# A builder that schedules the TensorE stream, with four PSUM banks shared by all tasks, in a kernel of four interleaved layers

## The chip, the cores and the metric

The kernel runs on one core of one Trainium2 chip. The metric is the device time of one execution, in microseconds (us); smaller is better. Engines are named as in the profile: PE is TensorE (PEld its weight loads), ACT is ScalarE, DVE is VectorE, POOL is GpSimd, SP issues transfers. Ratios are taken to runs of the kernel before on the same chip in the same rounds. The experiments ran on three chips, on which the kernel before took 3972, 3964 and 3957 us, so stage times of different traces, and medians, can differ by 0.4% for that reason alone.

## The reference, cut to what matters

The reference is four residual layers over 2048 rows of 512: A, B, A, B, each behind a layer norm.

```python
x = x + A(layernorm(x)); x = x + B(layernorm(x))
x = x + A(layernorm(x)); x = x + B(layernorm(x))

# A: 64 segments of 32 rows, 32 heads of 128, a memory of 8 rows handed on
for s in range(64):
    h = concat([mem, xs])                     # 40 rows
    q, k, v = h @ Wq, h @ Wk, h @ Wv          # each 32 heads x 128
    o = softmax(mask(q k^T * scale)) v @ Wo
    mem = o[:8]; outs.append(o[8:])           # the next segment needs mem

# B: full attention, 32 heads of 16, 2048 x 2048 scores a head
o = softmax(q k^T * 0.25) v @ wo
```

A segment of A is a chain that ends in the memory of the next, so there are 128 segments one after the other. A layer B has no such chain: as soon as A has left a few hundred rows, some of B's scores can be computed. The kernel cuts B into *units* (4 to 16 score matmuls, the exp, as many matmuls with V) and puts them between the tasks of the A segments. Units that are left when A has ended form a *tail*; between the two A layers a short *interlude* waits for B.

## The kernel before

One segment is 22 tasks in a fixed order. Q and K are projections of eight heads each, V of 1024 columns, S the scores and their exp, T the transposed probabilities, P the product with V, W the output projection. Each task fills one PSUM bank (P fills two, and all four W one), and an engine then copies the bank to SBUF. The Trainium skill, "PSUM — Partial Sum Buffer" (Specifications (TRN2)), gives eight banks of 512 fp32 values a partition; the pools below add up to eight (2 + 3 + 2 + 1).

```python
def psum_main(self, st):
    ...
    self.psA = self.pool("psA", bufs=2, space=PSUM)              # A tasks, projections: two banks
    psS = self.pool("psS", bufs=1, space=PSUM)
    self.SX = psS.tile([128, 3, 512], f32, name="b_SX")          # score columns 0 to 2 of a unit
    self.SY = [psS.tile([128, 512], f32, name=f"b_SY{i}") for i in range(2)]   # column 3
    self.oacc = psS.tile([128, 512], f32, name="b_oacc")

def psum_tail(self, st):                                         # layout of the tail
    ...
    self.psA = self.pool("psT", bufs=1, space=PSUM)
    self.SH = [psS.tile([128, 2, 512], f32, name=f"b_SH{i}") for i in range(3)]
    ...

def emit_qk(self, u):                                            # a unit: scores, then exp
    ...
    if self.tail:
        h = [self.SH[(2 * n) % 3], self.SH[(2 * n + 1) % 3]]
        ex = [(0, 2, h[0][:, 0:2, 0:w]), (2, 4, h[1][:, 0:2, 0:w])]
    else:
        y = self.SY[n % 2]
        ex = [(0, 3, self.SX[:, 0:3, 0:w]), (3, 4, y[:, 0:w])]
    ...

PLAN = "Q0 K0 Q1 K1 S0 Q2 K2 Q3 K3 S1 V0 V1 V2 T0 V3 T1 P0 P1 W0 W1 W2 W3".split()

def segment(self, A, s):
    quota = min(13, -(-self.backlog // 4)) if s % 4 == 0 else self.quota   # units in this segment
    self.act_evac = quota < 6        # light: Q, V and half of P copied by ACT, else by DVE
    for step in self.PLAN:
        ...                          # emit the task, then a unit or other work when it is due
```

Of the kernel before, what the change touches and what calls it, by code (L numbers as in the profile page):

```python
# [18 lines left out]
SEG = 32  # L19
M = 8  # L20
# [10 lines left out]
FORCE_GENERAL = False  # L31


class Kern:
    def __init__(self, ctx, tc, T):
        self.ctx, self.tc, self.nc, self.T = ctx, tc, tc.nc, T
        self.misc, self.outq, self.tqq = deque(), deque(), deque()
        self.runs, self.next = [], deque()
        self.cur = None
        self.pending = []  # L40
        self.backlog = 0
        self.acc_wait, self.acc_open = deque(), 0
        self.n_units = 0
        self.k_cache, self.v_cache = {}, {}
        self.act_evac = True
        self.tail = False
# [100 lines left out]
    def psum_main(self, st):  # L147
        self.ctx, outer = st, self.ctx
        self.psA = self.pool("psA", bufs=2, space=PSUM)
        psS = self.pool("psS", bufs=1, space=PSUM)  # L150
        self.SX = psS.tile([128, 3, 512], f32, name="b_SX")
        self.SY = [psS.tile([128, 512], f32, name=f"b_SY{i}") for i in range(2)]
        self.oacc = psS.tile([128, 512], f32, name="b_oacc")
        self.nc.vector.memset(self.oacc[:], 0.0)
        self.ctx = outer

    def psum_tail(self, st):
        self.ctx, outer = st, self.ctx
        self.tail = True
        self.psA = self.pool("psT", bufs=1, space=PSUM)  # L160
        psS = self.pool("psU", bufs=1, space=PSUM)
        self.SH = [psS.tile([128, 2, 512], f32, name=f"b_SH{i}") for i in range(3)]
        self.oacc = psS.tile([128, 512], f32, name="b_oaccT")
        self.nc.vector.memset(self.oacc[:], 0.0)
        self.ctx = outer
# [18 lines left out]
    def set_flag(self):  # L184
        nc = self.nc
        ps = self.psA.tile([1, 128], f32, name="flagT", tag="a")
        nc.tensor.transpose(ps[:], self.okm[:], self.identf[:])
        m = self.sm_p.tile([1, 1], f32, name="flagm")
        nc.vector.tensor_reduce(m[:], ps[:], axis=AX.X, op=ALU.min)
        nc.vector.tensor_scalar(m[:], m[:], -1.0, 1.0, op0=ALU.mult, op1=ALU.add)  # L190
        nc.vector.tensor_copy(self.flag[:], m[:])
# [16 lines left out]
    def transposes(self, xn, name):  # L208
        pt = self.psA.tile([128, 4, 128], bf16, name=name, tag="a")
        for ft in range(4):  # L210
            self.nc.tensor.transpose(pt[:, ft, :], xn[:, ft * 128:(ft + 1) * 128], self.ident[:])
        return pt


    def run_misc(self):
        if len(self.tqq) > 2 and self.tqq[0] is None:
            self.tqq.popleft()
        for q in (self.tqq, self.outq, self.misc):
            if q:
                f = q.popleft()  # L220
                if f is not None:
                    f()
                    return

    def flush_out(self):
        while self.outq:
            f = self.outq.popleft()
            if f is not None:
                f()
# [14 lines left out]
    def slot(self, unit=True):  # L244
        u = None
        if unit:
            self.commit()
            if self.next:
                u = self.next.popleft()
                self.backlog -= 1  # L250
                self.emit_qk(u)
                self.pending.append(u)
        if u is None and self.backlog == 0 and self.pending:
            self.pv_run()
        elif len(self.pending) >= 3:
            self.pv_run()
        self.run_misc()
        self.commit()
        for nu in list(self.next)[0:4]:
            self.load(nu)  # L260
        return u is not None

    def emit_qk(self, u):
        nc = self.nc
        self.load(u)
        assert u.run.q is not None and u.k is not None
# [4 lines left out]
        n = self.n_units  # L271
        self.n_units += 1
        if self.tail:
            h = [self.SH[(2 * n) % 3], self.SH[(2 * n + 1) % 3]]
            out = [h[0][:, 0, :], h[0][:, 1, :], h[1][:, 0, :], h[1][:, 1, :]]
            ex = [(0, 2, h[0][:, 0:2, 0:w]), (2, 4, h[1][:, 0:2, 0:w])]
        else:
            y = self.SY[n % 2]
            out = [self.SX[:, 0, :], self.SX[:, 1, :], self.SX[:, 2, :], y[:]]
            ex = [(0, 3, self.SX[:, 0:3, 0:w]), (3, 4, y[:, 0:w])]  # L280
# [4 lines left out]
        for a, b, src in ex:  # L285
            dst = pt[:, a:b, 0:w] if b - a > 1 else pt[:, a, 0:w]
            nc.scalar.activation(dst, src, ACT.Exp, scale=B_SCALE)  # L287

    def pv_run(self):
        u = self.pending.pop(0)  # L290
        self.pv_mm(u)
        if not u.last and self.pending:
            u = self.pending.pop(0)
            self.pv_mm(u)

    def pv_mm(self, u):
        qw = u.run.qw
        nj = len(u.kjs)
        for j, kj in enumerate(u.kjs):
# [3 lines left out]
        if u.last:  # L303
            u.run.close()

    def load(self, u):
        nc = self.nc
        run = u.run
        B = run.B
        if run.q is None:  # L310
            run.q = self.qp.tile([128, 512], bf16, name="b_q")
# [4 lines left out]
        if u.k is None:  # L316
# [15 lines left out]
            for w in run.units:  # L332
                if w.piece == u.piece:
                    w.k, w.v = self.k_cache[key], self.v_cache[key2]
# [8 lines left out]
    def drain_until(self, cond):  # L343
        while not cond():
            assert self.backlog or self.misc or self.outq or self.tqq or self.pending
            self.slot()


    def ln_chunk(self, x_src, ck, dt):
# [5 lines left out]
        def pe():  # L355
            pt = self.transposes(xn, "a_lnT")
            r0 = (4 * ck) % RING
            nc.vector.tensor_copy(self.hT[:, :, L * r0:L * (r0 + 4)].rearrange("p f (g q) -> p f g q", q=L)[:, :, :, 0:SEG],
                                  pt[:].rearrange("p f (g q) -> p f g q", q=SEG))
        return pe  # L360

    def qk_group(self, h_s, proj, g, ft_major=False):
        nc = self.nc
        W = self.Wq if proj == 0 else self.Wk
        ps = self.psA.tile([128, 8, L], f32, name="a_qk", tag="a")
        order = [(u, ft) for ft in range(4) for u in range(8)] if ft_major else [(u, ft) for u in range(8) for ft in range(4)]
        for n, (u, ft) in enumerate(order):
            h = 8 * g + u
            nc.tensor.matmul(ps[:, u, :], lhsT=W[:, ft, h * DH:(h + 1) * DH], rhs=h_s[:, ft, 0:L],  # L369
                             start=(n == 0) if ft_major else (ft == 0), stop=(ft == 3), skip_group_check=ft_major)  # L370
        if proj == 0:
            dst = self.QT[:, 8 * L * g:8 * L * (g + 1)].rearrange("p (u q) -> p u q", q=L)
            if self.act_evac:
                nc.scalar.copy(dst, ps[:])  # L374
            else:
                nc.vector.tensor_copy(dst, ps[:])  # L376
        else:
            nc.vector.tensor_copy(self.KT[:, 8 * g:8 * g + 8, :], ps[:])  # L378

    def v_round(self, h_s, r):  # L380
        nc = self.nc
        ps = self.psA.tile([128, 512], f32, name="a_v", tag="a")
        for ft in range(4):
            for ct in range(2):
                n = 2 * r + ct
                nc.tensor.matmul(ps[64 * ct:64 * ct + 64, :], lhsT=h_s[:, ft, :], rhs=self.Wv[:, ft, n * 512:(n + 1) * 512],  # L386
                                 start=(ft == 0), stop=(ft == 3), tile_position=(0, 64 * ct))
        if self.act_evac:
            nc.scalar.copy(self.V[:, r, :], ps[:])  # L389
        else:  # L390
            nc.vector.tensor_copy(self.V[:, r, :], ps[:])  # L391

    def s_group(self, s, st):
        nc = self.nc
        ps = self.psA.tile([128, 8, L], f32, name="a_s", tag="a")
        for hp in range(8):
            for ct in range(2):
                h = 2 * (8 * st + hp) + ct
                nc.tensor.matmul(ps[64 * ct:64 * ct + 64, hp, :], lhsT=self.QT[:, L * h:L * h + 64], rhs=self.KT[:, h, :], start=True, stop=True, tile_position=(0, 64 * ct))  # L399
        pn = self.pn[:, st, :, 0:L]  # L400
        nc.scalar.activation(pn, ps[:], ACT.Exp, scale=A_SCALE)  # L401
        nc.vector.tensor_tensor(self.pn[:, st, :, 0:SEG], self.pn[:, st, :, 0:SEG], self.mask[:], ALU.mult)
        sm = self.smA[:, s % 16, 8 * st:8 * st + 8]
        nc.vector.reduce_sum(sm, pn, axis=AX.X)
        r = self.sm_p.tile([128, 8, 1], f32, name="a_r")
        nc.vector.reciprocal(r[:, :, 0], sm)
        nc.vector.tensor_tensor(pn, pn, r[:].to_broadcast([128, 8, L]), ALU.mult)

    def pt_group(self, pti):
        nc = self.nc  # L410
        ps = self.psA.tile([128, 8, L], f32, name="a_pt", tag="a")
        for ii in range(8):
            r, h4 = divmod(8 * pti + ii, 4)
            for ct in range(2):
                h = 4 * (2 * r + ct) + h4
                hp, cs = divmod(h, 2)
                nc.tensor.matmul(ps[64 * ct:64 * ct + 64, ii, :], lhsT=self.pn[:, hp // 8, hp % 8, :], rhs=self.sel[cs], start=True, stop=True, tile_position=(0, 64 * ct))
        nc.vector.tensor_copy(self.PT[:, pti, :, :], ps[:])  # L418

    def pv_group(self, gi):  # L420
        nc = self.nc
        ps = [self.psA.tile([128, 8, L], f32, name=f"a_o{ct}", tag="a") for ct in range(2)]
        for r2 in range(2):
            for h4 in range(4):
                for ct in range(2):
                    r = 2 * gi + r2
                    nc.tensor.matmul(ps[ct][:, 4 * r2 + h4, :], lhsT=self.V[64 * ct:64 * ct + L, r, h4 * DH:(h4 + 1) * DH],  # L427
                                     rhs=self.PT[64 * ct:64 * ct + L, gi, 4 * r2 + h4, :], start=True, stop=True, tile_position=(64 * ct, 0))
        dst = self.OT[:].rearrange("p (gi r2 ct h4) q -> p gi ct r2 (h4 q)", gi=2, r2=2, ct=2, h4=4)
        for ct in range(2):  # L430
            src = ps[ct][:].rearrange("p (r2 h4) q -> p r2 (h4 q)", r2=2)
            if self.act_evac and ct == 0:
                nc.scalar.copy(dst[:, gi, ct], src)  # L433
            else:
# [524 lines left out]
```

## Time and profile before

The median is 3958.68 us (two runs, 3954.38 to 3962.97). The profiled execution took 3960.5 us.

The first lines are from the page: busy time and share of the span by engine, busy tenths of PE in 40 equal slices, the granted PE clock in tenths, and the chain of work that ended last.

```profile
PE 3268.9 (83%) x85249; PEld 2394.6 (60%) x85249; DVE 1781.1 (45%) x4190; ACT 2388.6 (60%) x3065; POOL 370.2 (9%) x621
...
PE   3888888888888888877888888888888888887777
...
PEclk9999999899899999968999999999999998997565
...
PE 54%; ACT 17%; issue 13%; DVE 12%; DMA 3%; POOL 1%; SPq 0%; ACTq 0%; POOLq 0%; DVEq 0%
```

PE is the busiest engine, but it is at 8 tenths nearly everywhere and in no slice at 9 (90% or more), and it holds only 54% of the chain. Something makes it wait a little all the time. The list of waits of the whole run names it. Its columns are the tile that PE was to write, the instruction it waited for, the total in us, the number of waits and the longest.

```profile
PE b_SX L283 <- ACT b_pt L287: 97.1, 200, 1.6
PE a_s L399 <- DVE a_KT L378: 65.3, 168, 1.9
...
PE a_wo L441 <- DVE a_OT L435: 37.2, 55, 2.9
PE a_o L427 <- DVE a_PT L418: 28.8, 84, 0.7
PE a_o L427 <- ACT a_OT L433: 27.0, 50, 0.6
PE a_v L386 <- ACT a_V L389: 25.6, 53, 0.9
```

Some lines are left out; one of them holds the only long waits (`a_lnT <- ln_xn`, 58.0 us in three waits, nearly all of it before the first segment). No other wait is long. `a_o <- a_OT` and `a_v <- a_V`: the second P cannot start before the copy of the first P has ended, a V round cannot start before the copy of the V two banks earlier has ended. The PE timeline at the end of a segment without units shows how they come in a row (start, length, what, idle time before it):

```profile
217.11 1.05 PE L386 MATMUL a_v<-a_Wv,a_hT 128*64 128x512 bf16 x8 [0.49 <-ACT a_V L389]
217.97 0.43 PE L417 MATMUL a_pt<-c_ident,a_pn 128*64 128x40 bf16 x16
218.89 0.45 PE L427 MATMUL a_o<-a_PT,a_V 40*128 40x40 bf16 x16 [0.49 <-ACT a_V L389]
219.90 0.40 PE L427 MATMUL a_o<-a_PT,a_V 40*128 40x40 bf16 x16 [0.56 <-ACT a_OT L433]
220.87 4.11 PE L441 MATMUL a_wo<-a_OT,a_Wo 128*128 128x40 bf16 x128 [0.56 <-ACT a_OT L433]
225.26 0.51 PE L369 MATMUL a_qk<-a_hT,a_Wq 128*128 128x40 bf16 x14 [0.28 <-DVE a_hT L486]
```

Four gaps of 0.49 to 0.56 us follow each other in little over 4 us. V3 and both P must wait for the copy two banks back, and W0 waits for the copy that empties a bank of the second P. The Trainium skill, "Perfetto Trace Analysis" (Identifying Performance Opportunities), says of gaps that repeat on an engine that should be saturated that they can mean too little SBUF or PSUM for the next tile. This trace agrees: all four gaps are in 22 of the 27 segments without units (the other five also project rows for B, and have three).

The next lines are stretches of the same segment (span, busy time of each engine with instructions, then the PE clock, the DMA share and GB/s):

```profile
213.60:217.00 3.40, 3.02 (x47) 1.91 (x42) 1.81 (x5) 2.13 (x4) 0.00 (x0) 1.00 0.02 5
217.00:220.40 3.40, 2.15 (x56) 1.72 (x56) 1.16 (x4) 1.08 (x4) 0.00 (x0) 1.00 0.00 0
220.40:223.80 3.40, 2.93 (x89) 2.93 (x89) 0.46 (x1) 0.41 (x1) 0.00 (x0) 0.52 0.02 5
```

The clock is at one half for one stretch, and in it lies most of the W projection: its 128 matmuls took 4.11 us here. Half the clock is not twice the time for these small matmuls: over the whole trace, W matmuls follow each other every 25.2 ns at full clock and every 33.6 ns at half clock, a third slower.

In the trace the clock changes only at multiples of 3.41 us. Of the 889 such windows that ran at full clock, all 57 with PE busy under 60% were followed by half clock, none of the 686 over 76%, and 53 of the 146 between.

By stage, from the trace (a segment is taken from one copy of its output to the next; a segment's units are half the exp instructions that start in it, as a unit has two; the first segment of each layer is left out):

| kernel before, segments with | number | mean us | PE busy | ACT busy | PE clock |
|---|---|---|---|---|---|
| no units | 27 | 21.4 | 18.0 | 6.0 | 0.93 |
| 4 or 5 units | 14 | 24.8 | 20.9 | 14.4 | 0.93 |
| 8 or 9 units | 8 | 27.4 | 24.0 | 16.4 | 0.94 |
| 12 units | 10 | 30.9 | 26.9 | 24.1 | 0.97 |
| 13 or 14 units | 35 | 32.6 | 27.6 | 26.0 | 0.94 |

The plain segment without units (no rows to project for B in it) takes 20.2 us. The last A segment ends at 3607.3 us; the interlude takes 113.3 us, the tail 353.2 us for 157 units.

### The profile page before, as it was taken

How to read it: one execution, taken by the hardware profiler on the slowest of the kernel's cores; microseconds unless marked ns; L12 is line 12 of the kernel's file. 1: busy time of each engine (PE TensorE's matmuls, PEld its weight loads, DVE VectorE, ACT ScalarE, POOL GpSimd, SP SyncE). 2: the span in 40 equal slices, each digit the busy share in tenths (PEclk: the TensorE clock that was granted, in tenths of full speed). 3: DMA queues.
4: the chain of work that ended last, by engine and by line, in shares of the span. 5: the costliest groups of instructions: out<-in, count | busy, mean ns of one | idle time of the engine just before them, and what ended most of it. 6: DMA issues, size and time to landing. Idle time of an engine off the chain costs nothing.

```text
span 3960.5 us, 184774 instructions
## 1 busy us (share of the span) xinstructions
PE 3268.9 (83%) x85249; PEld 2394.6 (60%) x85249; DVE 1781.1 (45%) x4190; ACT 2388.6 (60%) x3065; POOL 370.2 (9%) x621
## 2 busy tenths in 40 slices
PE   3888888888888888877888888888888888887777
PEld 3777767675666565644566675767566666555242
DVE  2333444545354544535545445454545444553311
ACT  1222354448676688875684226444867667878697
POOL 0000001111011110100100000011101111111010
PEclk9999999899899999968999999999999998997565
DMA  5000111213232334443331111121424233434342
GB/s 199 14 14 14 30 44 52 72 55 117 69 117 71 112 100 140 125 115 102 114 100 31 38 33 47 44 83 48 129 71 117 78 108 96 143 118 117 115 137 68
DMA packets 317745, 336.50 MB, mean 85 GB/s; under 512 B 93216, under 2 KB 250400, under 8 KB 316960
## 3 DMA queue, kind: packets, MB, share of 16 engines
q1 hardware_dynamic: 278800, 221.01, 20.0%
q0 software_dynamic: 32384, 94.68, 7.4%
q8 instruction: 668, 10.94, 1.1%
q10 hardware_dynamic: 5776, 8.91, 0.7%
q14 instruction: 117, 0.96, 0.1%
HBM read 229.81 MB, written 94.63 MB: 82 GB/s over the span
## 4 chain that ended last, share of the span: by engine, by line
PE 54%; ACT 17%; issue 13%; DVE 12%; DMA 3%; POOL 1%; SPq 0%; ACTq 0%; POOLq 0%; DVEq 0%
PE a_qk L369 16%; ACT b_pt L287 14%; PE a_wo L441 10%; PE a_v L386 9%; PE b_SX L283 6%; PE b_oacc L301 4%; DVE a_KT L378 2%; PE a_o L427 2%; PE a_s L399 2%; DVE a_OT L435 1%; ACT a_V L389 1%; ACT a_OT L433 1%; PE b_vps L643 1%; DVE a_V L391 1%; PE b_SH L283 1%
## 5 line engine op out<-in xcount | busy, mean ns | idle before, releaser
L287 ACT ACTIVATE b_pt<-b_SX 128x1536 bf16<-128x1536 f32 (+2 forms) x892 | 1284.1, 1440 | 590.4 <-PE b_SY L283 564.7
L386 PE MATMUL a_v<-a_Wv,a_hT 128*64 128x512 bf16 x4096 | 512.9, 382 | 70.9 <-ACT a_V L389 25.6
L441 PEld LDWEIGHTS <-a_Wo 128*128 128x128 bf16 x16384 | 498.3, 103 | 117.9 <-issue 109.5
L441 PE MATMUL a_wo<-a_OT,a_Wo 128*128 128x40 bf16 x16384 | 515.7, 189 | 57.6 <-DVE a_OT L435 37.2
L369 PE MATMUL a_qk<-a_hT,a_Wq 128*128 128x40 bf16 x16384 | 497.8, 180 | 36.2 <-DVE a_hT L486 21.3
L287 ACT ACTIVATE b_pt<-b_SY 128x512 bf16<-128x512 f32 (+2 forms) x892 | 526.2, 590 | 0.0
L369 PE MATMUL a_qk<-a_hT,a_Wk 128*128 128x40 bf16 x16384 | 494.8, 180 | 36.1 <-DVE a_QT L376 15.6
L369 PEld LDWEIGHTS <-a_Wq 128*128 128x128 bf16 x16384 | 460.6, 96 | 82.0 <-issue 70.6
L369 PEld LDWEIGHTS <-a_Wk 128*128 128x128 bf16 x16384 | 457.1, 96 | 83.5 <-issue 71.6
L283 PE MATMUL b_SX<-b_q,b_k 32*128 32x128 bf16 (+2 forms) x5616 | 377.2, 284 | 102.6 <-ACT b_pt L287 97.1
L283 PEld LDWEIGHTS <-b_k 32*128 32x128 bf16 x8832 | 199.9, 98 | 330.6 <-issue 285.3
L378 DVE CAST a_KT<-a_qk 128x320 bf16<-128x320 f32 x512 | 249.3, 487 | 330.6 <-PE a_qk L369 330.0
L386 PEld LDWEIGHTS <-a_hT 128*64 128x64 bf16 x4096 | 241.9, 110 | 233.9 <-issue 108.1
L283 PE MATMUL b_SY<-b_q,b_k 32*128 32x128 bf16 (+2 forms) x1872 | 370.3, 284 | 0.0
L301 PE MATMUL b_oacc<-b_pt,b_v 128*17 128x128 bf16 (+2 forms) x7472 | 306.6, 285 | 4.5 <-DVE b_ain L554 2.6
L287 ACT ACTIVATE b_pt<-b_SH 128x1024 bf16<-128x1024 f32 (+2 forms) x296 | 261.0, 1084 | 45.5 <-PE b_SH L283 45.4
L374 ACT CAST a_QT<-a_qk 128x320 bf16<-128x320 f32 x240 | 102.1, 426 | 223.6 <-PE a_qk L369 222.5
L427 PE MATMUL a_o<-a_PT,a_V 40*128 40x40 bf16 x4096 | 124.8, 179 | 134.7 <-DVE a_PT L418 28.8
L401 ACT ACTIVATE a_pn<-a_s 128x320 bf16<-128x320 f32 x256 | 112.6, 440 | 193.2 <-PE a_s L399 192.7
L301 PEld LDWEIGHTS <-b_v 128*17 128x17 bf16 x8832 | 140.8, 95 | 144.5 <-issue 112.6
L435 DVE CAST a_OT<-a_o 128x320 bf16<-128x320 f32 x392 | 179.6, 487 | 106.1 <-PE a_o L427 106.0
L559 POOL DMA_DIRECT2D b_A<-b_aout x208 | 113.1, 544 | 1212.0 <-DVE b_aout L545 1207.4
(96 smaller groups left out, 3107.3 us busy)
## 6 DMA issues: line engine op xcount, KB each, us to landing
b_ain<-b_A SPq DMA_DIRECT2D x224, 256.0 KB, 2.7
b_A<-b_ain POOLq DMA_DIRECT2D x176, 256.0 KB, 2.7
b_k<-b_K SPq DMA_DIRECT2D x320, 128.0 KB, 2.4
b_q<-b_Q SPq DMA_DIRECT2D x240, 128.0 KB, 2.5
b_v<-b_V SPq DMA_DIRECT2D x448, 68.0 KB, 2.3
b_A<-b_aout POOLq DMA_DIRECT2D x192, 64.0 KB, 2.3
x_after_a<-a_xo POOLq DMA_DIRECT2D x32, 256.0 KB, 3.6
b_Q<-b_qst POOLq DMA_DIRECT2D x32, 256.0 KB, 3.4
```

What stands on the lines that cost most here:

```text
L283: nc.tensor.matmul(out[t][:, j * qw:(j + 1) * qw], lhsT=k[32 * t:32 * t + 32, kj * 128:(kj + 1) * 128], rhs=q[32 * t:32 * t + 32, 0:qw], s ...
L287: nc.scalar.activation(dst, src, ACT.Exp, scale=B_SCALE)
L301: self.nc.tensor.matmul(self.oacc[32 * t:32 * t + 17, 0:qw], lhsT=u.v[:, kj, 17 * t:17 * t + 17], rhs=u.p[:, t, j * qw:(j + 1) * qw], star ...
L369: nc.tensor.matmul(ps[:, u, :], lhsT=W[:, ft, h * DH:(h + 1) * DH], rhs=h_s[:, ft, 0:L], start=(n == 0) if ft_major else (ft == 0), stop=( ...
L374: nc.scalar.copy(dst, ps[:])
L378: nc.vector.tensor_copy(self.KT[:, 8 * g:8 * g + 8, :], ps[:])
L386: nc.tensor.matmul(ps[64 * ct:64 * ct + 64, :], lhsT=h_s[:, ft, :], rhs=self.Wv[:, ft, n * 512:(n + 1) * 512], start=(ft == 0), stop=(ft = ...
L401: nc.scalar.activation(pn, ps[:], ACT.Exp, scale=A_SCALE)
L427: nc.tensor.matmul(ps[ct][:, 4 * r2 + h4, :], lhsT=self.V[64 * ct:64 * ct + L, r, h4 * DH:(h4 + 1) * DH], rhs=self.PT[64 * ct:64 * ct + L, ...
L435: nc.vector.tensor_copy(dst[:, gi, ct], src)
L441: self.nc.tensor.matmul(ps[:, ft, :], lhsT=self.Wo[:, h, 128 * ft:128 * ft + 128], rhs=self.OT[:, h, :], start=(h == 0 and ft == 0), stop= ...
L559: nc.gpsimd.dma_start(B.Acc_d[self.qc][self.hg][:, self.qo:self.qo + self.qw], acc[:, w])
```

## The change

The intent is that PE always has something ready. The builder keeps a clock of its own for PE, ACT and DVE, gives every task and unit a ready time, and at each step emits something that is ready: other work, a pair of V products, a unit, or one of the next four A tasks. Each copy goes to the engine that would end it first. The two banks of the A tasks and the two of the fourth score column become one list of four, from which every task and unit takes its bank. Units are spread thinner (backlog/8 a segment and at most 12, where it was backlog/4, fixed for four segments, and at most 13). The tail's own layout is dropped. The core of the diff, with cuts marked by dots:

```diff
     def psum_main(self, st):
-        self.psA = self.pool("psA", bufs=2, space=PSUM)
-        psS = self.pool("psS", bufs=1, space=PSUM)
-        self.SX = psS.tile([128, 3, 512], f32, name="b_SX")
-        self.SY = [psS.tile([128, 512], f32, name=f"b_SY{i}") for i in range(2)]
-        self.oacc = psS.tile([128, 512], f32, name="b_oacc")
+        ps = self.pool("psS", bufs=1, space=PSUM)
+        self.SX = ps.tile([128, 3, 512], f32, name="b_SX")
+        self.oacc = ps.tile([128, 512], f32, name="b_oacc")
+        self.static_banks(ps, 4)
...
-    def psum_tail(self, st):
...
+    def take(self):
+        b = min(self.banks, key=lambda b: b.free)
+        at, b.free = b.free, INF
+        return b, at
+
+    def evac_engine(self, n, ready):
+        ck = self.ck
+        end = {e: max(ck.t[e], ready + 0.04) + ck.cost(e, n) for e in ("ACT", "DVE")}
+        return "ACT" if end["ACT"] + self.act_bias < end["DVE"] else "DVE"
...
     def emit_qk(self, u):
-        if self.tail:
...
+        y, at = self.take()
+        done = ck.pe(0.25, max(at, self.x_free, u.at, u.run.at), "S")
+        out = [self.SX[:, 0, :], self.SX[:, 1, :], self.SX[:, 2, :], y.t[:]]
...
-    PLAN = "Q0 K0 Q1 K1 S0 Q2 K2 Q3 K3 S1 V0 V1 V2 T0 V3 T1 P0 P1 W0 W1 W2 W3".split()
+    PLAN = "Q0 K0 Q1 K1 S0 Q2 K2 Q3 K3 S1 T0 V0 V1 P0 V2 V3 T1 P1 W0 W1 W2 W3".split()
+    def a_pick(self, left):
+        now = self.ck.t["PE"] + 0.05
+        best = (INF, None)
+        for x in left[0:4]:
+            t = self.a_ready(x[0], int(x[1]), left)
+            if t <= now:
+                return t, x
...
+    def quota(self, A, s):
+        q = -(-self.backlog // 8)
...
+        return min(q, 12)
```

The emitted order of a segment without units becomes Q0 K0 Q1 K1 Q2 S0 K2 Q3 K3 T0 V0 S1 V1 V2 V3 P0 T1 W0 P1 W1 W2 W3: there is other work between each task and the one that needs its result.

## The prediction

> **What bounds it now.** The page gives TensorE 83% busy, ScalarE 60%, VectorE 45%, yet no engine is full for long. The run is 128 dependent A segments with B units (scores, exp, PV) strewn among them, then a B-only tail.
> - Segments without B units (timeline, 200 to 225 us) repeat every 20.2 us. Summing issue intervals from that timeline (32 Q, K or W matmuls 0.80 us, a V round 0.87, S or T 0.27, P 0.32, 0.11 per change of array tiling) gives 15.5 us of TensorE work. The list of waits between 200 and 400 us shows what is missing: a_s for the K copy (0.35 us, twice a segment), a_o and a_wo for the OT copies (0.56 each), a_v for the V copy (0.49), the seam a_qk for a_hT (0.28): about 3.3 us a segment, plus a pipeline drain at each wait.
> - B-heavy segments (1400 to 1700 us) take 30.2 us with 13 units. TensorE issue is about 24.7 us; ScalarE is busy 26 (exp of one unit 1.45 + 0.59 us). Waits are spread: b_SX for exp, a_s, a_o, a_wo.
> - Over all segments but the interlude the excess over TensorE issue time is about 5.9 us each, some 740 us in all.
> - The tail (3610 to 3960 us, 156 units) is ScalarE-bound: 99% busy between 3800 and 3900 at granted clock 0.50.
>
> **What the change does.** The instruction order (built, not run) has the same TensorE work; only order and banks change. After K1 comes Q2 before S0, T0 sits between K3 and S1, all V before P0, W0 between P0 and P1: each former wait has 0.3 to 1.6 us of ready work in it. Four shared banks let a task start while two others are evacuated. Copies go to the engine that ends first: light segments put nearly all on ScalarE (8.2 us of it, from 6.0), VectorE falls from 7.0 to 4.6. The seam stays, but B units fill it where there are any. B units are spread by backlog/8 instead of backlog/4, so light segments get 3 to 8 instead of 0 to 5, heavy ones 10 to 12 instead of 13; there ScalarE needs 24 to 27 us and becomes the limit.
> Against it: the tail grows from 156 to 181 units, and loses its own layout (three double banks) for the single SX of the main stage. The interlude near 1715 us shows that layout with the clock low: 2.21 us a unit, of which 2.04 is exp.
>
> **Sum (estimates from these durations).** Excess 5.9 to about 3.0 us a segment: -365 us. ScalarE-bound heavy segments: +30. Tail: 181 x about 2.25 + 10 against 353: +60. Interlude, 43 to 36 units: -10. 3959 - 285 = about **3670 us**, range 3560 to 3790. Chances: faster by over 2% 0.93, within 2% 0.05, slower 0.02.
>
> **What would show it.** Segments without units near 17.5 us; waits of a_s, a_o, a_wo and a_v mostly gone; TensorE share near 88 to 90% before the tail; last A segment ending near 3250 us (3607 now); tail near 415 us; ScalarE over 90% in 12-unit segments.
>
> **What would make it wrong.** The builder's clock may misplace tasks: one late copy in the in-order ScalarE queue (behind a 2 us exp) stalls TensorE, so the excess stays at 4 to 5 us. The tail could run at 2.5 us a unit. The clock: the Trainium skill, "TensorE: Matmul & The Clock Gate" (The HAM clock gate), says that an idle window of about 3.4 us halves it; the trace agrees in kind (0.50 in the tail, 0.92 to 1.00 in segments). A denser stream might lift it, for a gain of at most about 0.6 us a segment.

## The result, and the profile after

The kernel with the change takes 3589.98 us (median of two runs, 3589.69 to 3590.26). The ratio to the kernel before is 0.9069, 95% interval 0.9026 to 0.9111.

The same lines of the page after (span 3587.9 us):

```profile
PE 3112.4 (87%) x85206; PEld 2281.5 (64%) x85249; DVE 1594.7 (44%) x3887; ACT 2522.1 (70%) x3367; POOL 369.9 (10%) x621
...
PE   4999999999998898788899999999998898877555
...
PEclk9999999999999998789999999999999999866555
...
PE 73%; ACT 12%; issue 8%; DVE 4%; DMA 3%; SPq 0%; POOL 0%; ACTq 0%; DVEq 0%; POOLq 0%
```

PE now holds 73% of the chain, DVE 4% instead of 12%. PE's busy *time* also fell, by 157 us, with the same weight loads (85249); the reasons come below. The waits of PE after (all banks have one name here; L487 is V, L550 is W):

```profile
PE b_SX L388 <- ACT b_pt L390: 269.7, 277, 1.6
...
PE bank L487 <- DVE a_V L221: 15.6, 36, 1.2
...
PE bank L550 <- DVE a_OT L221: 9.0, 30, 1.3
```

The waits for copies are nearly gone; the wait of a unit for its SX tile has almost trebled. More than half of it, 147.6 us, lies in the tail, where the kernel before has other tiles (its wait `b_SH <- b_pt` is 46.0 us in the whole run); before the tail it grew from 91.4 to 122.1 us. The end of a segment without units on PE, for the same tasks as above:

```profile
185.73 1.46 PE L487 MATMUL bank<-a_Wv,a_hT 128*64 128x512 bf16 x12
187.13 0.37 PE L538 MATMUL bank<-a_PT,a_V 40*128 40x40 bf16 x16
187.42 0.43 PE L526 MATMUL bank<-c_ident,a_pn 128*64 128x40 bf16 x16
188.08 0.97 PE L550 MATMUL bank<-a_OT,a_Wo 128*128 128x40 bf16 x32 [0.22 <-DVE a_OT L221]
188.98 0.37 PE L538 MATMUL bank<-a_PT,a_V 40*128 40x40 bf16 x16
189.28 2.58 PE L550 MATMUL bank<-a_OT,a_Wo 128*128 128x40 bf16 x96
192.14 0.95 PE L472 MATMUL bank<-a_hT,a_Wq 128*128 128x40 bf16 x32 [0.28 <-DVE a_hT L644]
```

One gap of 0.22 us is left, and the seam to the next segment (0.28 us, as before). The plain segment takes 16.5 us at clock 1.00.

Where the time went, from the two traces. The 126 segments are those of the table above; PE idle is their length less PE's busy time:

| us | before | after | difference |
|---|---|---|---|
| first segment | 78.7 | 73.3 | -5 |
| 126 segments: PE busy | 2909 | 2771 | -138 |
| 126 segments: PE idle | 506 | 228 | -278 |
| interlude | 113.3 | 84.3 | -29 |
| tail (157 and 181 units) | 353.2 | 431.8 | +79 |
| span | 3960.5 | 3587.9 | -373 |

The -138 us has two main parts, reckoned from every matmul of the two traces (an estimate, against the mean time of the same kind of matmul at full clock). Matmuls that ran at half clock took some 125 us longer before and 45 after: about 80 us are the clock. And the last matmul before a gap is counted as busy until its modelled end, some 205 us in all before and 95 after: about 110 us belong to the removed waits. Some 50 us go the other way and are not explained. So about a fifth of the 416 us gained in the segments is the clock, the rest are removed waits with their ends, and a fifth of the sum is given back in the tail.

### The profile page after: what moved, and what is told of

It reads as the page before. It is cut to its first block, busy times and chain, and to the rows that moved or that the text cites. A ratio compares the mean times of both kernels' runs of the same rounds, so it can differ in the third digit from the quotient of the medians. Undisturbed runs are those within 1.5% of the kernel's fastest.

```text
span 3587.9 us, 186067 instructions
## 1 busy us (share of the span) xinstructions
PE 3112.4 (87%) x85206; PEld 2281.5 (64%) x85249; DVE 1594.7 (44%) x3887; ACT 2522.1 (70%) x3367; POOL 369.9 (10%) x621
## 4 chain that ended last, share of the span: by engine, by line
PE 73%; ACT 12%; issue 8%; DVE 4%; DMA 3%; SPq 0%; POOL 0%; ACTq 0%; DVEq 0%; POOLq 0%
PE bank L472 24%; PE bank L550 12%; PE bank L487 11%; ACT b_pt L390 10%; PE b_SX L388 10%; PE b_oacc L401 6%; PE bank L499 2%; PE bank L526 2%; PE bank L791 2%; PE bank L538 1%; DVE a_V L221 1%; PE bank L840 1%; PE bank L812 1%; DMA a_Wv<-in_A_Wv_dram 1%; ACT b_pt L391 1%
## 5 line engine op out<-in xcount | busy, mean ns | idle before, releaser
L390 ACT ACTIVATE b_pt<-b_SX 128x1536 bf16<-128x1536 f32 (+2 forms) x1040 | 1490.8, 1433 | 536.2 <-PE bank L388 487.8
L388 PE MATMUL b_SX<-b_q,b_k 32*128 32x128 bf16 (+1 forms) x6624 | 455.7, 292 | 281.7 <-ACT b_pt L390 269.7
L391 ACT ACTIVATE b_pt<-bank 128x512 bf16<-128x512 f32 (+2 forms) x1040 | 612.8, 589 | 0.5 <-PE bank L388 0.5
L472 PE MATMUL bank<-a_hT,a_Wq 128*128 128x40 bf16 x16384 | 509.7, 182 | 41.2 <-ACT a_QT L219 16.9
L487 PE MATMUL bank<-a_Wv,a_hT 128*64 128x512 bf16 x4096 | 509.7, 383 | 26.0 <-DVE a_V L221 15.6
L472 PEld LDWEIGHTS <-a_Wq 128*128 128x128 bf16 x16384 | 464.5, 97 | 95.3 <-issue 78.8
L472 PE MATMUL bank<-a_hT,a_Wk 128*128 128x40 bf16 x16384 | 506.7, 182 | 8.9 <-issue 4.8
L388 PEld LDWEIGHTS <-b_k 32*128 32x128 bf16 x8832 | 198.7, 99 | 464.2 <-issue 432.9
L550 PE MATMUL bank<-a_OT,a_Wo 128*128 128x40 bf16 x16384 | 475.7, 180 | 14.2 <-DVE a_OT L221 9.0
L472 PEld LDWEIGHTS <-a_Wk 128*128 128x128 bf16 x16384 | 459.7, 97 | 43.8 <-issue 36.4
L550 PEld LDWEIGHTS <-a_Wo 128*128 128x128 bf16 x16384 | 438.3, 96 | 58.0 <-issue 39.7
L401 PE MATMUL b_oacc<-b_pt,b_v 128*17 128x128 bf16 (+2 forms) x8832 | 440.0, 293 | 11.5 <-DVE b_ain L713 3.0
L388 PE MATMUL bank<-b_q,b_k 32*128 32x128 bf16 (+2 forms) x2208 | 445.9, 292 | 2.8 <-DVE b_xo L884 2.5
L487 PEld LDWEIGHTS <-a_hT 128*64 128x64 bf16 x4096 | 219.2, 110 | 195.5 <-issue 59.3
L401 PEld LDWEIGHTS <-b_v 128*17 128x17 bf16 x8832 | 155.3, 94 | 174.9 <-issue 139.6
L221 DVE CAST a_OT<-bank 128x320 bf16<-128x320 f32 x413 | 186.9, 485 | 132.9 <-PE bank L538 131.9
L219 ACT CAST a_V<-bank 128x512 bf16<-128x512 f32 x292 | 168.9, 597 | 61.4 <-PE bank L487 57.9
```

Source lines behind the costliest of these rows:

```text
L219: self.nc.scalar.copy(dst, src)
L221: self.nc.vector.tensor_copy(dst, src)
L388: nc.tensor.matmul(out[t][:, j * qw:(j + 1) * qw], lhsT=k[32 * t:32 * t + 32, kj * 128:(kj + 1) * 128], rhs=q[32 * t:32 * t + 32, 0:qw], s ...
L390: nc.scalar.activation(pt[:, 0:3, 0:w], self.SX[:, 0:3, 0:w], ACT.Exp, scale=B_SCALE)
L391: nc.scalar.activation(pt[:, 3, 0:w], y.t[:, 0:w], ACT.Exp, scale=B_SCALE)
L401: self.nc.tensor.matmul(self.oacc[32 * t:32 * t + 17, 0:qw], lhsT=u.v[:, kj, 17 * t:17 * t + 17], rhs=u.p[:, t, j * qw:(j + 1) * qw], star ...
```

## The experiments

The first theory was that of the prediction: what pays is the order that the scheduler finds, with the banks as a help. Its rivals were the four banks, the free choice of the copying engine and the new spread of units.

Some of these edits made the builder wait in a circle when built: an output chain held one of two scratch tiles while another waited for it. The cure, called the gate, lets such a chain start only while fewer than two scratch tiles are held. The first run measures the gate alone, and it is the control for all edits of the changed kernel.

### Control: the change with the gate

```diff
+            if c.gate == len(c.fns) and self.t_open >= 2:
+                continue
```

> Control. The changed kernel with one safety added to its builder: a chain that takes a scratch tile waits while two such tiles are open (without it several of the variants below cannot be built). Its TensorE order has the same number of B units in every stage (36 in the interlude, 181 in the tail). All theories: 3590 us within 1%. It is the kernel that the variants are compared with.

Measured: 3587.6 us (3584.96 to 3594.47), ratio 0.9046 (0.9022 to 0.9070), last A segment at 3154.2 us, tail 429.6 us. The gate costs nothing.

### The scheduler without its freedom of order

```diff
-    PLAN = "Q0 K0 Q1 K1 S0 Q2 K2 Q3 K3 S1 T0 V0 V1 P0 V2 V3 T1 P1 W0 W1 W2 W3".split()
+    PLAN = "Q0 K0 Q1 K1 S0 Q2 K2 Q3 K3 S1 V0 V1 V2 T0 V3 T1 P0 P1 W0 W1 W2 W3".split()
-        for x in left[0:4]:
+        for x in left[0:1]:
```

> A tasks in the order of the kernel before, no look-ahead; four shared banks, free choice of the copying engine, and ready times of B units and chains stay. Theory (the gain is the order, which puts ready A work into each wait): a segment without units goes from 16.5 to about 18 us, waits of a_s, a_o and a_wo come back, in all about 3690 us (3650 to 3740). Rival (four banks alone carry the gain): at most 3620 us.

Measured: 3570.78 us (3567.01 to 3579.70), ratio 0.9005 (0.8979 to 0.9031). With the A tasks in the order of the kernel before, the changed kernel is not slower but 0.4% faster than its control (ratios 0.9005 and 0.9046; the intervals overlap). Segments without units rise from 17.5 to 17.8 us, those with 10 or 11 units fall from 28.1 to 25.3. The first theory falls here: the freedom to order the A tasks is worth nothing over the whole run, once four banks are shared.

### Three shared banks instead of four

```diff
-        self.static_banks(ps, 4)
+        self.static_banks(ps, 3)
```

> Three shared banks instead of four, all else as in the control. Theory (order): little lost in light segments, 3600 to 3650 us. Rival (banks carry the gain): over 3750 us, with TensorE waits for copies in every segment.

Measured: 3898.41 us (3888.80 to 3901.04), ratio 0.9818 (0.9790 to 0.9845). One bank less gives back four fifths of the gain, with the scheduler and its ready times untouched. The waits of PE in this run (L543 is P, L492 is V, L477 is Q and K, L394 the second exp of a unit):

```profile
PE bank L543 <- ACT b_pt L394: 58.4, 43, 1.6
...
PE bank L492 <- ACT b_pt L394: 31.7, 55, 1.1
PE bank L555 <- DVE a_OT L222: 24.1, 51, 0.9
PE bank L477 <- ACT b_pt L394: 23.6, 49, 1.1
```

A tasks now wait for a unit's exp to leave its bank, which no line of the changed kernel's list shows at this size. Segments without units hardly suffer (17.9 us): there the order does stand in for a bank. Those with 12 units take 34.3 us (31.2 in the control).

### The copies on fixed engines, and the old spread of units

```diff
-        b.free = self.at["QK"[proj], g] = self.evac(dst, ps, 8 * L, done)
+        b.free = self.at["QK"[proj], g] = self.evac(dst, ps, 8 * L, done, "ACT" if proj == 0 and self.act_bias == 0 else "DVE")
 ...    # likewise V, T, P, the segment's output, b_kst and b_OT, as in the kernel before
```

> Each PSUM copy on the engine of the kernel before (Q, V and half of OT on ScalarE in light segments, the rest on VectorE). Theory (order): 3600 to 3650 us, light segments within 0.7 us of 16.5. Rival (choosing the engine that ends first carries the gain): over 3720 us.

Measured: 3690.94 us (3680.69 to 3700.29), ratio 0.9293 (0.9263 to 0.9323): 103 us over the control, between what the theory and what the rival expected.

```diff
-        quota = self.quota(A, s)
+        if s % 4 == 0:
+            self.quota4 = min(13, -(-self.backlog // 4))
+        quota = self.quota4
```

> The control (changed kernel, gated) with the rule of before for how many B units a segment takes (a quarter of the backlog at each fourth segment, at most 13; the tail has 160 units instead of 181). Theory: the spread of units is a small term, 3560 to 3620 us: heavier segments (13 units) cost about what the shorter tail saves. Rival (spreading over light segments is a large part of the gain): over 3650 us.

Measured: 3685.55 us (3683.80 to 3687.06), ratio 0.9293 (0.9269 to 0.9317), as the rival expected. The tail falls to 383.0 us, but the last A segment ends at 3302.4 us, as segments with 13 or 14 units take 35.7 us (clock 0.88).

Both parts matter inside the scheduler. That does not yet say that they are where the gain comes from: the next runs put parts of the change into the kernel *before*, which has the old copies and the old spread.

### Parts of the change in the kernel before

Only a new order, written into the fixed plan. It was meant to be the scheduler's, but is not quite: T0 stands one task too early, and W0 after P1:

```diff
-    PLAN = "Q0 K0 Q1 K1 S0 Q2 K2 Q3 K3 S1 V0 V1 V2 T0 V3 T1 P0 P1 W0 W1 W2 W3".split()
+    PLAN = "Q0 K0 Q1 K1 Q2 S0 K2 Q3 T0 K3 V0 S1 V1 V2 V3 P0 T1 P1 W0 W1 W2 W3".split()
```

> The kernel BEFORE with one line edited: its fixed list of A tasks gets an order that puts ready work into the waits (Q2 before S0, T0 before K3, V rounds before P0, T1 between P0 and P1). Two banks for A and two for the fourth score column stay, no scheduler. After the first runs showed that the new order is not needed where four banks are shared, theory 2 says order and banks stand in for each other in segments without units, and banks alone help where units run: order alone gives part, no-unit segments 18 to 19 us (20.2 before), 3780 to 3880 us in all. First theory (order is the gain): under 3700 us.

Measured: 3975.46 us (3973.13 to 3977.07), ratio 1.0024 (0.9998 to 1.0049). This order alone gives nothing, less than either expectation. It does what an order can do: the wait `a_s <- a_KT` (65.3 us before) falls to 4.3 us (waits for the Q copy, 27.0 us, come up in its place). The waits for banks stay, one is new (T1 now stands behind P0, which fills both banks: `a_pt <- a_OT`), and the hasty T0 and P bring new ones for data:

```profile
PE a_o L427 <- DVE a_PT L418: 63.7, 103, 1.5
...
PE a_pt L417 <- DVE a_OT L435: 53.3, 92, 0.9
...
PE a_pt L417 <- DVE a_pn L407: 29.2, 44, 0.9
PE a_v L386 <- ACT a_V L389: 28.2, 58, 0.7
```

Only the shared banks, an edit of three lines:

```diff
-        self.psA = self.pool("psA", bufs=2, space=PSUM)
+        self.psA = self.pool("psA", bufs=4, space=PSUM)
-        self.SY = [psS.tile([128, 512], f32, name=f"b_SY{i}") for i in range(2)]
...
-            y = self.SY[n % 2]
+            y = self.psA.tile([128, 512], f32, name="b_SY", tag="a")
```

> The kernel BEFORE with one change: the two banks of A and the two of the fourth score column become one pool of four, handed out in turn; order, fixed slots of B units and fixed copies stay. Theory 2 (banks carry most): no-unit segments 17.5 to 18.3 us, 3700 to 3800 us in all. Rival (ready times of B tasks, that is the scheduler itself, carry the gain where units run): no-unit segments gain, unit segments do not, over 3830 us.

Measured: 3560.86 us (3557.12 to 3562.09), ratio 0.8981 (0.8958 to 0.9004), better than either expectation. Three lines, with the old order, the old copies, the old spread and the old tail, give a little more than the whole change did (0.9046 for its control). The end of a segment without units in this run, in the old order:

```profile
192.99 1.06 PE L385 MATMUL a_v<-a_Wv,a_hT 128*64 128x512 bf16 x8
193.86 0.43 PE L416 MATMUL a_pt<-c_ident,a_pn 128*64 128x40 bf16 x16
194.22 0.37 PE L426 MATMUL a_o<-a_PT,a_V 40*128 40x40 bf16 x16
194.88 0.37 PE L426 MATMUL a_o<-a_PT,a_V 40*128 40x40 bf16 x16 [0.29 <-DVE a_PT L417]
195.18 3.38 PE L440 MATMUL a_wo<-a_OT,a_Wo 128*128 128x40 bf16 x128
```

Compare it with the six lines of the kernel before. All four waits for banks are gone, with the tasks in the same order. One shorter wait has come up that they had hidden, 0.29 us for data (the second P for its transposed probabilities). And the 128 W matmuls take 3.38 us instead of 4.11, as the clock is 1.00 here and was 0.50 for most of them there. Over the 126 segments PE idle is 267 us (506 before) and PE busy 2752 (2909 before).

Both at once:

> The kernel BEFORE with both edits of the two runs above, still no scheduler. Theory 2: within 40 us of the shared pool alone, as order adds little to four banks. If it comes near 3590 us, the scheduler itself is not needed; if it stays over 3700 us, the rest belongs to ready times, free choice of copies and the spread of units.

Measured: 3631.75 us (3628.55 to 3635.50), ratio 0.9161 (0.9136 to 0.9185). Theory 2 expected at most 40 us of difference; on top of the shared banks this fixed order costs 71 us: segments without units take 18.9 us (17.9 with the old order), and the waits are `a_o <- a_PT`, 73.0 us (18.9 with the old order), and `a_pt <- a_pn`, 31.4 us. That is the fault of these places of T and P, not of the scheduler, which puts K3 before T0. So these two runs judge one fixed order; for the scheduler's own order the run with its freedom taken away, above, is the better witness. The scheduler's exact order on two banks was not run.

So the second theory: the gain is the sharing of the banks.

### Is it sharing, or a third bank for the A tasks?

```diff
-        self.psA = self.pool("psA", bufs=2, space=PSUM)
+        self.psA = self.pool("psA", bufs=3, space=PSUM)
-        self.SY = [psS.tile([128, 512], f32, name=f"b_SY{i}") for i in range(2)]
+        self.SY = [psS.tile([128, 512], f32, name=f"b_SY{i}") for i in range(1)]
-            y = self.SY[n % 2]
+            y = self.SY[0]
```

> The kernel before with one line of banks changed: three banks for the A tasks alone, one for the fourth score column, nothing shared. Theory 2 as it stands (what pays is that all four banks are open to every task): segments without units gain most of what the shared pool gave (mean 18 to 18.5 us, against 21.4 before and 17.9 shared), as there no unit takes a bank anyway; the segments with 12 and 13 units gain little or lose (30 to 33 us, against 30.9 to 32.6 before and 29.3 to 30.0 shared), because a unit's fourth column must now wait for the last unit's second exp. Total 3650 to 3750 us. Rival (a third bank for A tasks is all that matters, sharing is only a means): total 3540 to 3590 us, as with the shared pool (3561).

Measured: 3752.11 us (3747.78 to 3753.83), ratio 0.9487 (0.9464 to 0.9509), 2 us above the range of the theory and far from the rival's. Same banks, same order; split 3 + 1 they give 5.1%, shared they give 10.2%. Segments without units took 18.7 us, a little over what was expected; those with 12 and with 13 or 14 units 31.0 and 32.9 us, no better than before, as expected (shared: 29.3 and 30.0). So in segments without units, where no unit competes for a bank, a third bank gives 2.6 of the 3.4 us and the number of banks is what counts; in the full segments the gain needs the sharing.

### The next wait of the shared pool: S for the K copy

```diff
-    PLAN = "Q0 K0 Q1 K1 S0 Q2 K2 Q3 K3 S1 V0 V1 V2 T0 V3 T1 P0 P1 W0 W1 W2 W3".split()
+    PLAN = "Q0 K0 Q1 K1 Q2 S0 K2 Q3 K3 V0 S1 V1 V2 T0 V3 T1 P0 P1 W0 W1 W2 W3".split()
```

(on top of the shared pool)

> The shared pool (before, four shared banks) with only its S tasks moved one task later (S0 after Q2, T0 and S1 later), the Q, K, V, P, W order as before. With the shared pool, the waits of a_s for the K copy came to 58.7 us in all. If those waits are the next limit, they go nearly to zero and the total is 3500 to 3540 us (3561 with the pool alone). If the rival holds (with the banks shared, the segment is at TensorE's own pace and what is saved at one wait is lost at the next), it is 3550 to 3575 us. The earlier mix of pool and the scheduler's whole static order gave 3632 us, so a worse result than 3575 would say that the order of V before S is the harm in it.

Measured: 3535.92 us (3533.54 to 3541.23), ratio 0.8937 (0.8915 to 0.8958), within the range. The line `a_s <- a_KT`, 58.7 us with the pool alone, is down to 0.7 us; segments without units take 17.3 us. Less than a third of the wait came through: about 17 us by the ratios (0.0044 of 3957). New waits, for the Q copy, took 28 us (18.4 for DVE, 10.0 for ACT).

### The tail

Why does the changed kernel (its control), which is ahead by 44 us of the shared pool when its last A segment ends (3154.2 and 3198.3 us), lose? Here are ScalarE's lines in the tail, of the kernel before and then of the kernel after:

```profile
3801.44 7.44 ACT L287 ACTIVATE b_pt<-b_SH 128x1024 bf16<-128x1024 f32 x8 [1.21 <-PE b_SH L283]
```

```profile
3399.72 1.45 ACT L390 ACTIVATE b_pt<-b_SX 128x1536 bf16<-128x1536 f32 x1 [0.27 <-PE bank L388]
3401.07 0.59 ACT L391 ACTIVATE b_pt<-bank 128x512 bf16<-128x512 f32 x1
3401.94 1.45 ACT L390 ACTIVATE b_pt<-b_SX 128x1536 bf16<-128x1536 f32 x1 [0.27 <-PE bank L388]
3403.28 0.59 ACT L391 ACTIVATE b_pt<-bank 128x512 bf16<-128x512 f32 x1
```

Before, four units of two exps each fill 7.44 us without a gap, 1.86 us a unit. After, a unit takes 2.22 us (3399.72 to 3401.94): with a single SX the next scores can only be written when the exp has left it, and ACT then waits 0.27 us for them. The Trainium skill, "ScalarE: Activation LUTs" (What ACT_TABLE_LOAD costs), gives 186 ns + 0.833 ns a column for an ACTIVATE with immediate scale and bias, and says that back-to-back ones overlap by about 93 ns. As an estimate from these figures that is 1.47 and 0.61 us for the two exps here (measured 1.45 and 0.59), and the trace agrees with an overlap of about that size: the second exp starts 0.10 us before the first has ended, and none is left where ACT waits for PE. The experiment puts the three double banks back for the tail:

```diff
+    def psum_tail(self, st):
+        ps = self.pool("psU", bufs=1, space=PSUM)
+        self.SH = [ps.tile([128, 2, 512], f32, name=f"b_SH{i}") for i in range(3)]
+        self.static_banks(ps, 1, "t")
...     # emit_qk uses SH in halves where it is there, with ready times
```

> The changed kernel's control (3588 us) with the tail layout of before (three score tiles of two banks, exp in halves), scheduler and order unchanged, still about 181 units in the tail. If the loss in the tail is the layout (2.21 us a unit with the single SX against 1.86 in the tail of before), the tail falls from 430 us to 345 to 385 us, the part before it stays at 3154 us within 10, and the total is 3500 to 3550 us. If the loss is only the number of units or the scheduler's choice between units and PV, the tail stays above 410 us and the total above 3565.

Measured: 3520.38 us (3515.04 to 3525.61), ratio 0.8903 (0.8878 to 0.8928). The tail falls by 50 us to 379.9 us, for the same 181 units, and ACT is busy 99.97 of the 100 us from 3300 us on:

```profile
3339.46 8.50 ACT L411 ACTIVATE b_pt<-b_SH 128x1024 bf16<-128x1024 f32 x9
```

Of the 79 us that the change lost in the tail, the layout is about 50; the rest goes with the 24 units more. The last A segment ends at 3134.3 us, 20 us earlier than in the control (expected: within 10 us of 3154). About 12 of the 20 would be the chip, an estimate: the kernel before took 3956.74 us there and 3972.04 in the control's rounds. The other 8 are within what the expectation allowed and were not looked into; the edit also moves the bank of the PV accumulator (the tile in which the products with V add up).

### The parts together

```diff
# fixed order of the A tasks, tail layout, and
-        q = -(-self.backlog // 8)
+        q = -(-self.backlog // 4)
-        return min(q, 12)
+        return min(q, 10)
```

> Three edits of the scheduler together, a try for the fastest version: the fixed order of before (3571 us alone), the tail layout of before, and units by backlog/4 but at most 10 a segment, so that no units are left over for the seam between two segments, as there are in the segments of 12. If the three add: fixed order -17, tail about -55, no leftovers at the seam: 3490 to 3530 us. If the cap only moves units into the tail (175 units), about 3520 to 3550.

Measured: 3460.98 us (3456.62 to 3462.51), ratio 0.8747 (0.8725 to 0.8768), better than the range expected and the fastest of all kernels here. Why the cap at 10 units: in the changed kernel, segments with 12 had units left when their last W was emitted, and these ran at the seam, each waiting for SX, while the next segment stood ready. PE's lines of such a seam in the kernel after (L388 scores, L401 the products with V, L472 the next Q):

```profile
1061.37 0.39 PE L388 MATMUL b_SX<-b_q,b_k 32*128 32x512 bf16 x3
...
1063.37 0.39 PE L388 MATMUL b_SX<-b_q,b_k 32*128 32x512 bf16 x3 [1.17 <-ACT b_pt L390]
...
1065.36 0.40 PE L388 MATMUL b_SX<-b_q,b_k 32*128 32x512 bf16 x3 [1.13 <-ACT b_pt L390]
...
1067.36 0.61 PE L388 MATMUL b_SX<-b_q,b_k 32*128 32x512 bf16 x3 [0.92 <-ACT b_pt L390]
...
1067.91 0.78 PE L472 MATMUL bank<-a_hT,a_Wq 128*128 128x40 bf16 x18
```

Six us pass with PE mostly idle, and the clock falls to 0.50 at 1066 us, in time for the next segment's projections. With the cap, the wait `b_SX <- b_pt` is 69.3 us (118.9 with the tail layout alone), segments with 10 or 11 units take 25.6 us at clock 0.99 (28.1 in the control, at 0.97), and PE is busy 90% of the span:

```profile
PE 3121.1 (90%) x85201; PEld 2286.8 (66%) x85249; DVE 1620.9 (47%) x3966; ACT 2460.5 (71%) x3288; POOL 370.3 (11%) x621
```

By the ratios, the fixed order took 0.0041 and the tail 0.0143 off the control's 0.9046; the sum would be 0.8862, an estimate that assumes they add. The other 0.0115 (45 us) would be the new spread, or the parts together. The spread with the cap was not run alone, so that split is an estimate.

### All results

| kernel | us, median | ratio to before | 126 segments: PE busy + idle, clock | tail |
|---|---|---|---|---|
| before | 3958.68 | 1 | 2909 + 506, 0.936 | 353 |
| after | 3589.98 | 0.9069 | 2771 + 228, 0.972 | 432 |
| control (after with gate) | 3587.60 | 0.9046 | 2772 + 225, 0.972 | 430 |
| after, fixed order | 3570.78 | 0.9005 | | 429 |
| after, three banks | 3898.41 | 0.9818 | 2898 + 408, 0.939 | 431 |
| after, fixed copies | 3690.94 | 0.9293 | | 426 |
| after, old spread | 3685.55 | 0.9293 | | 383 |
| before, new order only | 3975.46 | 1.0024 | | 355 |
| before, shared banks only | 3560.86 | 0.8981 | 2752 + 267, 0.989 | 357 |
| before, both | 3631.75 | 0.9161 | | 355 |
| before, banks split 3 + 1 | 3752.11 | 0.9487 | 2870 + 328, 0.973 | 358 |
| before, shared banks, S late | 3535.92 | 0.8937 | 2757 + 245, 0.982 | 359 |
| after, tail layout | 3520.38 | 0.8903 | 2767 + 212, 0.972 | 380 |
| after, fixed order, tail, cap 10 | 3460.98 | 0.8747 | 2741 + 191, 0.988 | 370 |

Busy time times clock is no measure of the work in this table: half clock costs the W matmuls a third, not double, and busy time holds the modelled ends before waits. It comes to 2694 to 2728 us in the rows where waits and half clock rise and fall together, and to 2794 us in the split 3 + 1, which has less half clock than the kernel before but as much busy time before gaps (some 205 us by the estimate above).

## Why the prediction was right or wrong

**The number.** 3670 us was predicted, 3560 to 3790 as range; 3590 came out, inside it and 80 us below the point. The call of "faster by over 2%" was right.

**The step that failed: what carries the gain.** The prediction says: "After K1 comes Q2 before S0, T0 sits between K3 and S1, all V before P0, W0 between P0 and P1: each former wait has 0.3 to 1.6 us of ready work in it." It put the order first and named the four banks as the second thing, without a share for each. The runs show the reverse: the shared banks alone 0.8981, an order close to the scheduler's alone 1.0024, and the changed kernel with the old order no slower than with the new. The list of waits had said as much: `a_o <- a_OT` and `a_v <- a_V` wait for a bank, not for data, and with the changed order on two banks the wait of V for its bank was still 28.2 us (25.6 before). The prediction read these lines as gaps to be filled with other work; but other work needs a bank too: P0 takes both, so that T1, put between P0 and P1 on two banks, waited 53.3 us in all. As the change brings order and banks together, the number did not depend on which of them carries the gain; that it came out in the range although this step failed is luck.

**The term left out of the sum: the clock.** The prediction reckoned -365 us for the segments, gave back 30 in the heavy ones, and put the clock among the risks, "for a gain of at most about 0.6 us a segment". Measured, the 126 segments fell by 416 us. About 80 us of it are the clock by the estimate above, 0.6 us a segment: the bound was right, and it was reached. The other 336 us are close to the net 335 that the prediction gave the waits. So the point was missed by about the size of the clock; the interlude (19 us better than predicted) and the tail (19 us worse) offset each other, which is luck. Where the prediction went wrong is in treating the clock as a chance apart: it looked for an idle window of 3.4 us, but windows with PE busy under 60% were enough, and removing the gaps removed most of them (up to the end of the last A segment the clock fell to half 109 times in the kernel before and 33 times in the kernel after). Its range for the clock in the segments, 0.92 to 1.00, was also too high; stretches of 100 us read 0.88 to 0.98 between 100 and 1700 us.

**Heavy segments.** The prediction had ACT over 90% busy in segments with 12 units and as their limit. It was 25.0 of 31.1 us, 80%. Neither engine was full: the seam lines show units waiting one after the other for the single SX tile. A second SX tile was not tried, so that it would cure this is not shown. There are also fewer such segments than before (about 20 with 12 or more, 45 before), because units moved to lighter segments and to the tail.

**The tail.** 415 us predicted, 432 measured; 2.21 us a unit was read rightly from the interlude, but 181 units of it are only 400 us (an estimate from that duration), and what comes besides them took some 32 us where the prediction allowed 10. That the layout is most of the loss, and not the number of units alone, was foreseen in kind ("loses its own layout") and is shown by the run with the tail layout: 50 us.

**The signs that were named.** Segments without units near 17.5 us: 17.4 in the mean, 16.5 for the plain ones that took 20.2. Waits of a_s, a_o, a_wo and a_v mostly gone: so it was. PE at 88 to 90% before the tail: 90.4% (2851.5 of 3156.1 us; before the change 3005.7 of 3607.3 us, 83.3%). Last A segment near 3250 us: 3156 us, earlier by what the clock and the interlude gave (29 us instead of 10). A builder's clock that misplaces tasks, the main risk named, did no visible harm in the light segments.

**What the scheduler is worth.** As shipped, nothing over three changed lines (0.9046 against 0.8981), because what it gains before the tail it loses in it: it leaves 24 more units there and gives each 0.35 us more. With the tail's layout back it is ahead by 0.8% (0.8903 against 0.8981), and with the cap and the fixed order by 2.3% (0.8747). Against the pool with S one task later (0.8937) the first of these is not clear of noise. Which of its parts earn that is only half shown: going back on the free choice of engine or on the new spread costs about 100 us each inside the scheduler, and neither was tried on top of the shared pool.

## What to carry to other kernels

Before ordering work around a wait, ask whether it is for data or for a buffer; if the engine waits for the copy that empties a bank, try first to let all users draw from one pool of banks, for a fixed split lets one user wait while the other's bank is empty. Then look at the clock: here many gaps of half a microsecond cost twice, as idle time and as slower work at half clock after it. When a change drops a special layout for one stage, cost that stage by itself; here a tenth of the span took back a fifth of the gain.

## What the Trainium skill lacked or had wrong

- "TensorE: Matmul & The Clock Gate" (Why this matters for your kernels) advises against idle gaps above about 3 us. Here gaps far shorter were enough: after 3.40 us with PE busy 2.15 us and no gap over 0.56 us, the clock was at one half for about 3.4 us; and again after the seam with gaps of 0.9 to 1.2 us. A stretch with 3.02 us busy of 3.40 was not followed by it. By the estimate above, less half clock is worth about 80 us of the 416 gained in the segments. Of the 3.41 us windows of the kernel before that ran at full clock, all 57 with PE busy under 60% were followed by half clock and none of 686 over 76%; between, other things decide that these traces do not show. The same page's section "A second HAM failure mode: psum-queue depth-cycling" describes this case (short idle times between groups, for PSUM banks, let the clock swing) but gives no size for it. That the clock has two states, half and full, and a window of about 3.4 us (What's actually happening), agrees with this trace: it reads 1.00 or 0.50 wherever a stretch lies within one state, and all its changes lie on a grid of 3.41 us.
- "Perfetto Trace Analysis" (Identifying Performance Opportunities) is right that repeated gaps can mean too little PSUM. Its later sections tell to rotate matmul groups through banks and to use all eight, as both kernels do, but neither it nor "PSUM — Partial Sum Buffer" says how to divide them between users. Here the same four banks gave 3959 us split 2 + 2, 3752 us split 3 + 1 and 3561 us shared.
- "ScalarE: Activation LUTs" agrees within 4% for single exps (1.45 and 0.59 us measured, 1.47 and 0.61 estimated by its formula). What it does not say is what becomes of it when the next exp has to wait for its tile to be filled: eight exps of 128x1024 took 7.44 us from three tiles in turn, while a unit of the same size with one large tile took 2.22 us instead of 1.86.
